# Attention and two feed-forward layers on one Trainium2 core: score and value matmuls chained in written order, transposes placed ahead of scores

## The chip, the core and the metric

The kernel runs on one core of one Trainium2 chip. The metric is the time of one execution on the device in microseconds (us), the median over a few runs. TensorE (PE) does the matmuls and the transposes and loads its weights beside them (PEld). VectorE (DVE), ScalarE (ACT) and GpSimd (POOL) do the elementwise work, and SyncE (SP) issues the DMAs.

## The reference

Three layers follow one another; each takes the output of the one before.

```python
# q, k, v: (4 batches, 8 heads, 576 positions, 64); positions of a batch see the last 128
scores = scale * np.matmul(q, k.transpose(0, 1, 3, 2))
mask = (rel >= 0) & (rel < 128)
scores = np.where(mask, scores + bias, -1e9)          # bias: slope of the head * distance
attn = np.exp(scores - max); attn = attn / (sum + 1e-9)
x = np.matmul(attn, v)                                # -> (2304 tokens, 512)
h = x @ w_in;  g = h * sigmoid(1.702 * h);  x = g @ w_out              # 512 -> 2048 -> 512
g = x @ w_gate; x = (g * sigmoid(g) * (x @ w_val)) @ w_out2            # 512 -> 1536 -> 512
```

## The kernel before

The 2304 tokens are 18 tiles of 128, taken in five blocks j of 4, 2, 4, 4 and 4 tiles (`A_BLOCKS`). A block goes through attention and then through the first feed-forward layer. The second layer follows for all tokens when the last block is done.

**Attention.** The eight heads are taken as four pairs `hp`; the two heads e of a pair lie in rows 0 to 63 and 64 to 127 of the q and k tiles. A group g is two token tiles. A unit (j, hp, g) has these steps:

- `scores`: 8 matmuls (16 instructions in the trace, two for each f32 matmul) into two PSUM banks `sb`, one for each head. From block 1 on each uses 64 rows and 64 columns of TensorE's array: the head sets the row half, the half c of the token tile sets the column half, so that four matmuls can stand on the array side by side.
- `minima` (DVE: the mask in `fold`, L365, then bias and minimum, L443), `exponentials` (ACT, L468), `reciprocals` (DVE), `normalise` (POOL, L491). The result is the tile `prob`; there are three of it.
- `transposes`: 4 matmuls with the identity into one bank `pt` (L536). `apart` copies it to `pf` (ACT, L567) and masks it in two selects (POOL, L569 and L572). There is one `pf`.

After both groups of a pair comes `values`: 24 matmuls (48 instructions) of `pf` and v. In blocks 2 to 4 they too are quarters of the array (L605): the half r of the keys sets the row half and the bank (`xb`, two of them), the head sets the column half. `take_x` adds the two banks (ACT L647, DVE L648) and splits the sum into `xh` and `xl` (L649, L641). In block 1 one bank and whole keys are used (L617).

**First feed-forward layer.** For each of 16 steps f of a block, `h_part` does 12 wide matmuls (128 x 512; 128 x 256 in block 1) into a bank `hp`, and ACT and DVE make `gh` and `gl` of it (L688, L690, L696, L698). `y_part`, two steps later, does 12 wide matmuls into four banks `y`, which the block holds to its end. Of the eight PSUM banks the four others go round among hp, sb, pt and xb.

**What sets the order.** Block 0 and the start of its layer follow a list, `PLAN`. From there on a loop over (j, f) issues `h_part`, an event, `y_part`, an event; an event of block j+1's attention has a place in half steps of block j (`hooks`). A unit's scores, its transposes and its pair's values have places of their own, worked out from `SPREAD`, `TRANSPOSE_LAG`, `VALUES_LAG` and `APART`. The rest is left to a scheduler: it orders each engine's instructions by its own estimates of time and may move a matmul whose inputs or bank it believes late behind others. `tc.issue_after(x)` forbids it to put an instruction ahead of x. Before the change the scores are behind the last h and y matmuls (`scores_and_norm`), and the first matmul of each triple in `three` is behind the last score matmul; the matmuls of a score unit and those of a value unit are not tied to each other.

The preparation of the second layer's weights (DMA, ACT, DVE; `prepare`) is issued in small steps between, in blocks 1 to 4.

## Time and profile before

| | |
|---|---|
| time, median of 3 runs | 903.93 us (903.85 to 904.41) |
| the profiled execution | 905.12 us, of which the span that the trace shows is 903.4 us |
| PE busy in the span | 890.8 us, 99% |
| DVE busy | 673.1 us, 75% |
| ACT busy | 453.9 us, 50% |
| attention of blocks 1 / 2 / 3 / 4 on PE | 72 to 130 / 130 to 195 / 195 to 302 / 302 to 396 us |
| second layer on PE | from about 500 us to the end |

A row of PE's timeline gives start and length of an instruction or of a run of equal ones; consecutive lengths overlap, since matmuls are pipelined. Starts are what counts: a wide matmul of 512 columns follows the one before at 0.23 us. So what a small unit costs PE is the time from the start of the last wide matmul ahead of it to the start of the first one behind it, less 0.23 us. A row's `[0.39 <-DVE th L690]` is idle time before it and what ended it.

### The profile page before, as it was taken

The page shows a single profiled execution, that of the slowest core. Times are in us where ns is not written, and L with a number is a line of the kernel's source. Part 1 is how long each engine was busy: PE and PEld are TensorE (multiplying, and loading weights), DVE is VectorE, ACT ScalarE, POOL GpSimd, SP SyncE. Part 2 cuts the span into 40 slices and gives each one's busy share as a digit, 9 for nine tenths or more (in the row PEclk, how much of TensorE's full clock was granted, in tenths as well). Part 3 has the DMA queues.
Part 4 walks back from the last instruction along what each step waited for, and adds up shares of the span by engine and source line. Part 5 has one row for each costly group of instructions (what it writes and reads, how often), then busy time and mean ns, then how long its engine had stood idle before and what let it go on. Part 6 is the DMA issues. An engine that isn't in the chain of part 4 may idle for free.

```text
span 903.4 us, 15609 instructions
## 1 busy us (share of the span) xinstructions
PE 890.8 (99%) x5556; PEld 794.4 (88%) x5556; DVE 673.1 (75%) x1707; ACT 453.9 (50%) x1065; POOL 119.4 (13%) x218
## 2 busy tenths in 40 slices
PE   7999999999999999999999999999999999999998
PEld 5687779987778776788888999999999999999998
DVE  8988847657776777877658386669866779866777
ACT  7867636645654555645445354435444335344331
POOL 6301413404440133210000000000000000000000
PEclk9999999999999999999999999999999999999999
DMA  9961214436455474546774577687887787887764
GB/s 332 377 246 29 72 56 147 153 108 199 169 194 197 165 237 163 207 162 234 249 300 146 209 263 268 245 305 260 289 292 257 255 315 260 289 293 258 258 223 140
DMA packets 71309, 199.20 MB, mean 220 GB/s; under 512 B 6720, under 2 KB 37952, under 8 KB 64320
## 3 DMA queue, kind: packets, MB, share of 16 engines
q1 hardware_dynamic: 71232, 198.21, 62.5%
q8 instruction: 44, 0.72, 0.3%
q14 instruction: 33, 0.27, 0.1%
HBM read 155.71 MB, written 42.47 MB: 219 GB/s over the span
## 4 chain that ended last, share of the span: by engine, by line
PE 82%; DVE 7%; DMA 6%; ACT 2%; issue 2%; SPq 1%; POOL 0%; DVEq 0%; ACTq 0%
PE sx L816 17%; PE ox L816 8%; PE sz L816 8%; PE y L653 6%; PE hp L653 6%; PE y L654 5%; PE y L655 5%; PE hp L654 5%; PE hp L655 5%; PE oz L816 4%; PE sy L816 4%; PE oy L816 2%; DMA wraw<-in_moe_w_in 2%; PE xb L605 2%; PE sb L395 1%
## 5 line engine op out<-in xcount | busy, mean ns | idle before, releaser
L816 PE MATMUL sx<-ya,wg 128*128 128x384 f32 x864 | 172.4, 335 | 0.0
L816 PEld LDWEIGHTS sx<-ya,wg 128*128 128x128 f32 x864 | 151.9, 188 | 0.1
L653 PE MATMUL hp<-xh,wt 128*128 128x512 f32 (+1 forms) x320 | 120.9, 378 | 0.6 <-DVE stat L443 0.3
L653 PE MATMUL y<-gh,wt 128*128 128x512 f32 (+1 forms) x320 | 120.4, 379 | 0.0
L654 PE MATMUL hp<-xl,wt 128*128 128x512 f32 (+1 forms) x320 | 118.2, 369 | 0.9 <-DVE xl L641 0.8
L655 PE MATMUL y<-gh,wt 128*128 128x512 f32 (+1 forms) x320 | 118.6, 371 | 0.0
L654 PE MATMUL y<-gl,wt 128*128 128x512 f32 (+1 forms) x320 | 118.2, 369 | 0.0
L655 PE MATMUL hp<-xh,wt 128*128 128x512 f32 (+1 forms) x320 | 117.9, 368 | 0.0
L816 PE MATMUL ox<-p,wg 128*128 128x384 f32 x432 | 89.6, 337 | 0.0
L845 DVE TENSOR_TENSOR p<-th,p 128x384 fp32r<-128x384 f32 x126 | 67.9, 552 | 28.2 <-ACT p L844 27.6
L816 PE MATMUL sz<-ya,wg 128*128 128x384 f32 x432 | 88.8, 336 | 0.0
L491 POOL TENSOR_SCALAR prob<-prob,stat 128x128 f32<-128x128 f32 x112 | 58.6, 539 | 179.2 <-DVE stat L481 60.8
L844 ACT ACTIVATE p<-th 128x384 fp32r<-128x384 f32 x126 | 63.4, 521 | 36.1 <-DVE th L840 28.5
L698 DVE TENSOR_TENSOR gl<-th,gh 128x512 fp32r<-128x512 f32 (+1 forms) x80 | 52.3, 654 | 33.2 <-ACT gh L696 32.1
L816 PEld LDWEIGHTS ox<-p,wg 128*128 128x128 f32 x432 | 76.5, 188 | 0.0
L816 PEld LDWEIGHTS sz<-ya,wg 128*128 128x128 f32 x432 | 76.1, 188 | 0.1
L653 PEld LDWEIGHTS y<-gh,wt 128*128 128x128 f32 x320 | 60.2, 188 | 14.4 <-issue 3.7
L653 PEld LDWEIGHTS hp<-xh,wt 128*128 128x128 f32 x320 | 60.1, 188 | 13.7 <-issue 1.7
L851 ACT ACTIVATE th<-c 128x384 f32<-128x384 f32 x54 | 28.3, 524 | 86.9 <-DVE c L836 86.7
L696 ACT ACTIVATE gh<-th 128x512 fp32r<-128x512 f32 (+1 forms) x80 | 46.8, 585 | 49.4 <-PE y L655 32.5
L654 PEld LDWEIGHTS hp<-xl,wt 128*128 128x128 f32 x320 | 60.2, 188 | 11.5 <-DVE xl L641 2.0
L655 PEld LDWEIGHTS hp<-xh,wt 128*128 128x128 f32 x320 | 60.1, 188 | 10.6 <-DVE wt L231 0.2
(112 smaller groups left out, 1558.3 us busy)
## 6 DMA issues: line engine op xcount, KB each, us to landing
wg<-w_scratch SPq DMA_DIRECT2D x36, 1024.0 KB, 5.4
wg<-w_scratch SPq DMA_DIRECT2D x36, 768.0 KB, 5.1
wg<-wo_scratch SPq DMA_DIRECT2D x18, 1024.0 KB, 6.6
wg<-wo_scratch SPq DMA_DIRECT2D x18, 768.0 KB, 7.9
w_scratch<-wa SPq DMA_DIRECT2D x24, 512.0 KB, 2.7
w_scratch<-wb SPq DMA_DIRECT2D x24, 384.0 KB, 3.5
wraw<-in_moe_w_in SPq DMA_DIRECT2D x16, 512.0 KB, 9.1
wraw<-in_moe_w_out SPq DMA_DIRECT2D x16, 512.0 KB, 9.4
```

What stands on the lines that cost most here:

```text
L395: ins = nc.tensor.matmul(out=sb[e][c : c + size, (i % 2) * 256 + lo : (i % 2) * 256 + hi], lhsT=u["q"][rows, i * P + c : i * P + c + size] ...
L491: nc.gpsimd.tensor_scalar(out=of[x], in0=of[x], scalar1=stat[:, 3, x : x + 1], scalar2=1.0, op0=ALU.mult, op1=ALU.mult,)
L605: nc.tensor.matmul(out=x[r][e * D : (e + 1) * D, i * P + a : i * P + a + w], lhsT=u["v"][e][keys, kt + lead, :], rhs=u["pf"][keys].rearran ...
L653: nc.tensor.matmul(out=out_ap, lhsT=whi, rhs=xhi, start=start, stop=False)
L654: nc.tensor.matmul(out=out_ap, lhsT=whi, rhs=xlo, start=False, stop=False)
L655: marks[products] = nc.tensor.matmul(out=out_ap, lhsT=wlo, rhs=xhi, start=False, stop=stop).ins
L696: a = nc.scalar.activation(out=gh[:, :m], in_=th[:, :m], func=AF.Copy)
L698: d = nc.vector.tensor_tensor(out=gl[:, :m], in0=th[:, :m], in1=gh[:, :m].bitcast(F32), op=ALU.subtract)
L816: nc.tensor.matmul(out=bank_[:, :HT], lhsT=w[:, kk, at, a, :], rhs=p2[2 * (q // 2 - 1) + kk, i][:, b, :] if m == "O" else y2[q // NP2, i][ ...
L844: nc.scalar.activation(out=t[:, 0], in_=src, func=AF.Copy)
L845: nc.vector.tensor_tensor(out=t[:, 1], in0=src, in1=t[:, 0].bitcast(F32), op=ALU.subtract)
L851: nc.scalar.activation(out=th, in_=g, func=AF.Tanh, scale=0.5)
```

## The change

Seven edits:

1. `in_row` ties each score and each value matmul of blocks 1 to 4 behind the one issued before it in the same unit.
2. The scores take the heads in turn, 1 then 0; the values take the key halves (and so the banks) in turn, 1 then 0, and the key tiles from the last to the first.
3. The first matmul of each h and y triple (`three`) is put behind the last value matmul too, not only behind the last score matmul.
4. The values are put behind the last h and y matmuls issued before them, as the scores are.
5. In blocks 3 and 4 (`JOINED`) the transposes are too, and
6. all places of these blocks come from a table, `PLACES`, one entry for each of 32 half steps: S is a unit's scores, T its transposes, V a pair's values. Unit n's transposes stand just ahead of unit n+2's scores.
7. In block 2 the values come 1.6 steps of the plan after the transposes, where it was 0.95.

```diff
@@ -78,6 +78,13 @@
 SPREAD, LOAD_LAG, TRANSPOSE_LAG, VALUES_LAG, APART = 0.65, 0.3, 4.0, 0.95, 2.0
 
 LENGTHS = {1: 8, 2: 18}
+
+JOINED = 3, 4
+
+PLACES = (
+    "", "S0", "", "S1", "", "", "", "T0 S2", "", "T1 S3", "", "V0", "", "T2 S4", "", "T3 S5", "", "V1",
...
+)
 
 QUARTERS = 1, 2
 
@@ -373,6 +380,13 @@
 
         return range(2 * g, min(2 * g + 2, a_blocks[j][1]))
 
+    def in_row(j, prev, matmul, **kw):
+
+        if j == 0:
+            return matmul(**kw).ins
+        with tc.issue_after(prev) if prev is not None else nullcontext():
+            return matmul(**kw).ins
+
     def scores(j, hp, g):
 
 
@@ -383,6 +397,7 @@
         sb = [bank("sb") for _ in range(2)]
         quarters = j >= QUARTERS[0]
         size = D if quarters else P
+        ins = None
         for i in tiles:
             for c in range(0, P, size):
 
@@ -390,16 +405,19 @@
                 if c and kind(t0 + i) == "cross":
                     lo = P + D
                 hi = P + c + size
-                for e in range(2):
+                for e in range(2) if j == 0 else (1, 0):
                     rows = slice(e * D, (e + 1) * D)
-                    ins = nc.tensor.matmul(
+                    ins = in_row(
+                        j,
+                        ins,
+                        nc.tensor.matmul,
                         out=sb[e][c : c + size, (i % 2) * 256 + lo : (i % 2) * 256 + hi],
                         lhsT=u["q"][rows, i * P + c : i * P + c + size],
                         rhs=u["k"][rows, (i + lead - 1) * P + lo : (i + lead - 1) * P + hi],
                         start=True,
                         stop=True,
                         skip_group_check=quarters,
-                    ).ins
+                    )
         if j > 0:
             marks["sb"] = ins
         u["sb", g] = sb
@@ -584,7 +602,9 @@
         def row(e, i):
             return 2 * (4 * (i // 2) + e * len(tiles_of(j, i // 2)) + i % 2)
 
-        for kt in range(-lead, n):
+        order = range(-lead, n) if j == 0 else range(n - 1, -lead - 1, -1)
+        ins = None
+        for kt in order:
             qts = [i for i in (kt, kt + 1) if 0 <= i < n and (i == kt or kind(t0 + i) != "first")]
             if quarters:
 
@@ -597,31 +617,39 @@
                 together = len(qts) == 2 and kt % 2 == 0
                 for p in range(1 if together else len(qts)):
                     for e in range(2):
-                        for r in range(2):
+                        for r in (1, 0):
                             (i, own, a, b), last = parts[r][p], parts[r][-1 if together else p]
                             w = b - a if last[0] == i else P - a + last[3]
                             at = (row(e, i) + own) * P + a
                             keys = slice(r * D, (r + 1) * D)
-                            nc.tensor.matmul(
+                            ins = in_row(
+                                j,
+                                ins,
+                                nc.tensor.matmul,
                                 out=x[r][e * D : (e + 1) * D, i * P + a : i * P + a + w],
                                 lhsT=u["v"][e][keys, kt + lead, :],
                                 rhs=u["pf"][keys].rearrange("p x c -> p (x c)")[:, at : at + w],
-                                start=(kt == -lead and p == 0),
-                                stop=(kt == n - 1),
+                                start=(kt == order[0] and p == 0),
+                                stop=(kt == order[-1]),
                                 skip_group_check=True,
                             )
                 continue
             w = len(qts) * P
             for e in range(2):
                 rows = [row(e, i) + (i == kt) for i in qts]
-                nc.tensor.matmul(
+                ins = in_row(
+                    j,
+                    ins,
+                    nc.tensor.matmul,
                     out=x[0][e * D : (e + 1) * D, qts[0] * P : qts[0] * P + w],
                     lhsT=u["v"][e][:, kt + lead, :],
                     rhs=u["pf"][:, rows[0] : rows[-1] + 1 : max(1, rows[-1] - rows[0]), :],
-                    start=(kt == -lead),
-                    stop=(kt == n - 1),
+                    start=(kt == order[0]),
+                    stop=(kt == order[-1]),
                     skip_group_check=True,
                 )
+        if j > 0:
+            marks["xb"] = ins
         u["x"] = x
 
     def take_x(j, hp, lower):
@@ -649,7 +677,10 @@
         nc.scalar.activation(out=xh[:, hp, :m], in_=total[:, :m], func=AF.Copy)
 
     def three(products, out_ap, whi, wlo, xhi, xlo, start, stop):
-        with tc.issue_after(marks["sb"]) if "sb" in marks else nullcontext():
+        with ExitStack() as behind:
+            for row in ("sb", "xb"):
+                if row in marks:
+                    behind.enter_context(tc.issue_after(marks[row]))
             nc.tensor.matmul(out=out_ap, lhsT=whi, rhs=xhi, start=start, stop=False)
         nc.tensor.matmul(out=out_ap, lhsT=whi, rhs=xlo, start=False, stop=False)
         marks[products] = nc.tensor.matmul(out=out_ap, lhsT=wlo, rhs=xhi, start=False, stop=stop).ins
@@ -935,12 +966,17 @@
         normalise(*u)
 
     def transposed(*u):
-        transposes(*u)
+        if u[0] in JOINED:
+            with tc.issue_after(marks["h"]), tc.issue_after(marks["y"]):
+                transposes(*u)
+        else:
+            transposes(*u)
         for select in range(2):
             apart(*u, select)
 
     def values_and_x(j, hp):
-        values(j, hp)
+        with tc.issue_after(marks["h"]), tc.issue_after(marks["y"]):
+            values(j, hp)
         for lower in range(2):
             take_x(j, hp, lower)
 
@@ -1048,6 +1084,21 @@
 
         if j > 1:
             ev.append((at - 1, start))
+        if j in JOINED:
+            for n, place in enumerate(PLACES):
+                for what in place.split():
+                    h = int(what[1:])
+                    if what[0] == "V":
+                        ev.append((at + n, lambda h=h: values_and_x(j, h)))
+                        continue
+                    u = j, h // G, h % G
+                    if what[0] == "T":
+                        ev.append((at + n, lambda u=u: transposed(*u)))
+                        continue
+                    ev.append((at + n, lambda u=u: scores_and_norm(*u)))
+                    if h % G == G - 1 and h // G + 2 < H // 2:
+                        ev.append((at + n + 1, lambda h=h: load_pair(j, h // G + 2)))
+            return [(min(p, 2 * begin[j] - 1), e) for p, e in ev]
         begun, scored, valued = 0, 0, []
         for h in range(G * H // 2):
             u = j, h // G, h % G
@@ -1062,7 +1113,7 @@
             begun = max(begun, at + step * h + lag)
             ev.append((begun, lambda u=u: transposed(*u)))
             if last:
-                begun = begun + step * VALUES_LAG
+                begun = begun + step * (VALUES_LAG if j != 2 else 1.6)
                 valued.append(begun)
                 ev.append((begun, lambda u=u: values_and_x(*u[:2])))
         return [(min(p, 2 * begin[j] - 1), e) for p, e in ev]
```

On PE, the value unit of block 3's third pair before the change (xb_3326 is the bank of key half 0, xb_3327 that of half 1, pf the masked weights, y and hp the wide matmuls of the first layer):

```order
L605 MATMUL xb_3326<-pf_3133,vr_2635 64x64 [waits DMAHW0_49,DVE_49,Pool_49]
L605 MATMUL xb_3326<-pf_3133,vr_2635 64x192 [waits Pool_49]
L605 MATMUL xb_3326<-pf_3133,vr_2635 64x192
...
L605 MATMUL xb_3326<-pf_3133,vr_2635 64x128 x2
L653 MATMUL y_2659<-gh_3159,wt_842 128x512
...
L654 MATMUL y_2661<-gl_3160,wt_842 128x512
L605 MATMUL xb_3327<-pf_3133,vr_2635 64x128 [waits DVE_49,PE_49]
L605 MATMUL xb_3327<-pf_3133,vr_2635 64x192 x2
...
L605 MATMUL xb_3327<-pf_3133,vr_2635 64x64 x2
L536 MATMUL pt_3357<-ident_70,prob_3193 128x128 [waits DVE_49,PE_49,Pool_49]
```

All twelve matmuls of half 0 stand together, eight wide ones come, and then the twelve of half 1. The same unit with the change (xb_3392 is half 1, xb_3391 half 0):

```order
L686 MATMUL y_2653<-gh_3197,wt_836 128x512
L388 MATMUL xb_3392<-pf_3224,vr_2635 64x64 [waits DMAHW0_49,Activation_49,Pool_49]
L388 MATMUL xb_3391<-pf_3224,vr_2635 64x128 [waits DVE_49,PE_49]
L388 MATMUL xb_3392<-pf_3224,vr_2635 64x64 [waits DMAHW1_49]
L388 MATMUL xb_3391<-pf_3224,vr_2635 64x128
L388 MATMUL xb_3392<-pf_3224,vr_2635 64x192
L388 MATMUL xb_3391<-pf_3224,vr_2635 64x192
...
L388 MATMUL xb_3391<-pf_3224,vr_2635 64x64
L684 MATMUL hp_3429<-xh_1826,wt_1009 128x512 [waits DVE_49,PE_49]
```

The 24 stand together, the halves in turn, and the first waits for the last select on POOL and for both banks.

On PE, a score unit of block 4 before (sb_4264 and sb_4265 are the banks of its two heads):

```order
L655 MATMUL y_3897<-gh_4023,wt_704 128x512
L395 MATMUL sb_4264<-kr_3869,qr_3868 64x192 [waits DVE_49]
L395 MATMUL sb_4264<-kr_3869,qr_3868 64x192 x3
L395 MATMUL sb_4265<-kr_3869,qr_3868 64x192 [waits Activation_49]
L395 MATMUL sb_4265<-kr_3869,qr_3868 64x192 x3
L653 MATMUL y_3894<-gh_4112,wt_577 128x512
```

One head's four matmuls stand ahead of the other's. The same unit with the change, with the transposes (pt) that the table places there:

```order
L686 MATMUL y_3888<-gh_4105,wt_577 128x512
L554 MATMUL pt_4308<-ident_70,prob_4059 128x128 [waits Activation_49,Pool_49]
L554 MATMUL pt_4308<-ident_70,prob_4059 128x128 [waits Pool_49] x3
L388 MATMUL sb_4317<-kr_3869,qr_3868 64x192 [waits DVE_49,PE_49]
L388 MATMUL sb_4316<-kr_3869,qr_3868 64x192 [waits DVE_49,PE_49]
L388 MATMUL sb_4317<-kr_3869,qr_3868 64x192
L388 MATMUL sb_4316<-kr_3869,qr_3868 64x192
...
L388 MATMUL sb_4316<-kr_3869,qr_3868 64x192
L684 MATMUL y_3885<-gh_4191,wt_729 128x512
```

The transposes of the unit two before stand directly ahead, and the two heads come in turn. The matmuls of the second layer stand on PE in the same order before and after.

## Rows read from the trace of the kernel before

**Rows 1.** The page: busy time (part 1), shares of the chain that ended last (part 4).

```profile
PE 890.8 (99%) x5556; PEld 794.4 (88%) x5556; DVE 673.1 (75%) x1707; ACT 453.9 (50%) x1065; POOL 119.4 (13%) x218
...
PE 82%; DVE 7%; DMA 6%; ACT 2%; issue 2%; SPq 1%; POOL 0%; DVEq 0%; ACTq 0%
```

**Rows 2.** Windows by stage: length, busy us of PE, PEld, DVE, ACT, POOL; clock, DMA.

```profile
195.00:302.00 107.00, 106.61 (x737) 84.44 (x736) 78.44 (x257) 57.96 (x156) 31.44 (x48) 1.00 0.55 187
302.00:396.00 94.00, 91.75 (x657) 70.84 (x655) 73.61 (x250) 53.94 (x148) 27.15 (x48) 1.00 0.56 192
396.00:903.00 507.00, 503.84 (x2754) 484.51 (x2748) 370.27 (x739) 218.63 (x443) 0.00 (x0) 1.00 0.72 253
```

**Rows 3.** PE's timeline, two score units: start us, length us, line, out<-in, form, count.

```profile
195.67 0.88 PE L395 MATMUL sb<-kr,qr 64*64 64x192 f32 x16
...
349.59 0.39 PE L655 MATMUL y<-gh,wt 128*128 128x512 f32 x1
349.91 0.89 PE L395 MATMUL sb<-kr,qr 64*64 64x192 f32 x16
350.73 0.50 PE L653 MATMUL y<-gh,wt 128*128 128x512 f32 x1
```

**Rows 4.** PE's timeline, a score unit of block 3 with a late second head.

```profile
237.27 0.39 PE L655 MATMUL y<-gh,wt 128*128 128x512 f32 x1
238.05 1.45 PE L395 MATMUL sb<-kr,qr 64*64 64x192 f32 x16 [0.39 <-DVE th L690]
239.42 0.50 PE L653 MATMUL hp<-xh,wt 128*128 128x512 f32 x1
```

**Rows 5.** PE's timeline, a value unit of block 3 in one piece.

```profile
282.18 1.55 PE L605 MATMUL xb<-pf,vr 64*64 64x64 f32 x48
```

**Rows 6.** PE's timeline, a value unit of block 3 in two pieces.

```profile
264.29 1.54 PE L605 MATMUL xb<-pf,vr 64*64 64x64 f32 x24
...
267.82 1.53 PE L605 MATMUL xb<-pf,vr 64*64 64x128 f32 x24
```

**Rows 7.** Windows of the value matmuls L605 alone, blocks 2, 3 and 4.

```profile
130.00:195.00 65.00, 6.50 (x192) 5.16 (x192) 1.00 0.39 127
195.00:302.00 107.00, 8.20 (x192) 7.11 (x192) 1.00 0.55 187
302.00:396.00 94.00, 8.13 (x192) 7.06 (x192) 1.00 0.56 192
```

**Rows 8.** Windows of the score matmuls L395 alone, blocks 3 and 4.

```profile
195.00:302.00 107.00, 8.11 (x128) 5.00 (x128) 1.00 0.55 187
302.00:396.00 94.00, 7.82 (x128) 4.75 (x128) 1.00 0.56 192
```

**Rows 9.** PE's timeline, two places of block 1's attention.

```profile
109.30 1.09 PE L617 MATMUL xb<-pf,vr 128*64 128x128 f32 x12
110.32 0.66 PE L536 MATMUL pt<-ident,prob 128*128 128x128 f32 x4
...
114.56 0.44 PE L617 MATMUL xb<-pf,vr 128*64 128x128 f32 x4
114.93 0.66 PE L536 MATMUL pt<-ident,prob 128*128 128x128 f32 x4
115.52 0.87 PE L395 MATMUL sb<-kr,qr 64*64 64x192 f32 x8
116.31 0.87 PE L617 MATMUL xb<-pf,vr 128*64 128x256 f32 x8
...
117.91 0.50 PE L653 MATMUL y<-gh,wt 128*128 128x512 f32 x1
```

**Rows 10.** Transposes of block 4 on PE, and the last select of their copy (POOL).

```profile
337.88 0.66 PE L536 MATMUL pt<-ident,prob 128*128 128x128 f32 x4
...
345.62 0.63 POOL L572 TENSOR_SCALAR_AFFINE_SELECT pf<-pf 128x512 f32<-128x512 f32 x1
```

More of the change, by code (lines that the diff above doesn't have):

```diff
@@ L80 @@
 LENGTHS = {1: 8, 2: 18}
+JOINED = 3, 4
+PLACES = (
+    "", "S0", "", "S1", "", "", "", "T0 S2", "", "T1 S3", "", "V0", "", "T2 S4", "", "T3 S5", "", "V1",
+    "", "T4 S6", "", "T5 S7", "", "V2", "", "T6", "", "T7", "", "V3", "", "",
+)
 QUARTERS = 1, 2
```

## The prediction, made before the changed kernel ran

> **What bounds the kernel now.** I began with the page's busy times and its chain of waits. PE is busy for 890.8 of 903.4 us, and 82% of the chain that ended last are PE's own instructions; DVE comes next with 7% [rows 1]. So a change pays only where it shortens what PE does or the few waits in which PE stands still. Next the windows by stage: behind the last attention unit, from 396 us on, PE stands still for 3 of 507 us, and its order there isn't changed; the change acts in the attention of blocks 1 to 4. In block 3 PE idles for 0.39 us, in block 4 for 2.25 us [rows 2]. Little of the loss is idle time, then. The rest hides in "busy" PE, and only the timeline shows it: the small matmuls of one unit cost different times at different places.
>
> A score unit of 16 instructions lasts 0.88 or 0.89 us; it costs PE 350.73 - 349.59 - 0.23 = 0.91 us [rows 3]. Another, 237.27 to 239.42, costs 1.92 us: PE waited 0.39 us at its start, and then it lasted 1.45 us [rows 4]. A value unit of 48 instructions in one piece lasts 1.55 us [rows 5]. In two pieces of 24 the pieces last 1.54 and 1.53 us, as much each as the whole [rows 6]. A piece holds one key half, so it uses one row half of the array, and nothing stands on the other. That is what the reader is to see: the same count of instructions, and twice the time.
>
> **The change part by part.** No matmul is added or taken away. What changes is which ones stand side by side, and what waits.
>
> *Values of blocks 3 and 4 (edits 1 to 4).* All value matmuls of block 3 take 8.20 us, of block 4 8.13 us [rows 7]. Four whole units would take 4 x 1.55 = 6.20 us. That gives 2.00 + 1.93 = 3.9 us. Each block has one unit in two pieces; its second piece enters the small form once more, and a small unit begins 0.32 us after the wide matmul ahead of it (349.59 to 349.91) instead of 0.23 [rows 3], so 2 x 0.1 = 0.2 us more. Together 4.1 us. This gain is certain as far as the units stand together in the new order, and they do. The reversed key order costs nothing by itself: as many matmuls of the same widths.
>
> *Values of block 2.* 6.50 - 6.20 = 0.3 us [rows 7]; the last but one unit stands in three pieces, two entries more, 0.2 us. Together 0.5 us.
>
> *Block 1.* A value unit (4 of 12 instructions), transposes, 8 score instructions, the other 8 of the values, the other 8 of the scores take 117.91 - 114.56 = 3.35 us. The scores of one head alone take 0.79 us (115.52 to 116.31), as much as both together. Joined: values 1.02 (109.30 to 110.32), transposes 0.59 (114.93 to 115.52) [rows 9], scores 0.82 (349.91 to 350.73) [rows 3], in all 2.43 us. Gain 0.9 us.
>
> So far 4.1 + 0.5 + 0.9 = 5.5 us.
>
> *Scores: the heads in turn.* In 13 of the 28 units before, one head's matmuls stand ahead of the other's in the queue. That costs nothing as long as both banks are free: the unit at 349.91 is one of these, with 0.89 us, the one at 195.67 has the heads in turn, with 0.88 [rows 3]. I take 0. The Trainium skill ("TensorE: Matmul & The Clock Gate", Part 3, "What overlaps and what doesn't") says the opposite: "MATMULs are pc-monotone in start AND end — strict FIFO, no reordering", by which the second head couldn't start beside the first, and taking turns would be worth a lot. Here the trace disagrees with it, 0.89 against 0.88 us; it is the last rival below.
>
> *Waits that the old order has.* Score matmuls take 8.11 and 7.82 us in blocks 3 and 4 [rows 8], eight clean units 8 x 0.89 = 7.12: 0.99 + 0.70 = 1.7 us lie in units whose second head waited for its bank. With PE's idle 0.39 + 2.25 = 2.6 us [rows 2] there are 4.3 us of waiting.
>
> *Waits that the new order has.* Here the trace of before shows only neighbours. Each place in blocks 3 and 4 is fixed now, and PE takes its queue in order: behind a late unit stand the wide matmuls of h, which feed ACT and DVE. Four banks still serve hp, pt, sb and xb, so a score unit still asks for two banks that DVE has to give back; I let the 1.7 us stay. The transposes come six half steps behind their scores, some 17 us (a half step is 94 us / 32 = 2.9 us [rows 2]), and shouldn't wait. The values are new: their first matmul asks for the last select and both banks, where the old order began with what was there. Between the end of the transposes and the values now stand a score unit and 24 wide matmuls, 0.8 + 24 x 0.23 = 6.3 us. In the trace the select after the transposes at 337.88 ended at 346.25, 7.7 us behind their end [rows 10]. That was with other work ahead of the copy on ACT, and it would be 1.4 us late. The lower bound is 0. I take 0.1 us for each of 8 units, near the lower end, as the copy stands early on ACT in the new order: 0.8 us. New waits in all 1.7 + 0.8 = 2.5 us, between 0 and 1.7 + 12 x 1.4 = 18.5.
>
> *Transposes directly ahead of scores.* Only an entry into the small form could be spared, 0.1 us for each of 12 at most, while transposes followed by scores take 0.59 us [rows 9]. I take 0, bounds -1.2 and +1.2 us.
>
> *DMA.* The next pair's q, k and v are asked for at other places on SP, and the v load waits until the values have read the old tile; the raw weights queue behind it. Today that is hidden: the view of waits names no DMA among PE's in blocks 3 and 4, and DVE, which works on the raw weights, is busy for only 73.61 of 94 us [rows 2]. I take 0; if this cover is gone, the first layer's ACT work comes late, which is rival 2.
>
> **Sum.** -5.5 - 4.3 + 2.5 = -7.3 us. The profiled execution took 905.12 us, the span and 1.7 us around it; it is 1.2 us above the median of the runs, and I apply the difference to that median: 903.9 - 7.3 = 896.6 us.
>
> **The rivals.**
>
> 1. All waits go, as the table gives every step more time than it has now. For it: a late head is rare, 1.7 us over 16 units. Against it: no bank is added. 903.9 - 5.5 - 4.3 = 894.1 us.
> 2. DVE keeps what PE saves. It is busy for 78% of block 4's time; with 5 us less that is 83%, and in order. If half of the gain in blocks 3 and 4 (4.1 + 4.3 - 2.5 = 5.9 us) comes back as waits of PE, 899.6 us; if all of it, 902.5 us, and only blocks 1 and 2 have gained.
> 3. Slower: PE stands before the value units until the last select is done. If ACT's copy is as late as at 337.88, that is 1.4 us for each of 12 units, 17 us: 903.9 - 9.8 + 17 = 911 us. It decides from 9.8 / 12 = 0.8 us for each unit. For it: that row is no mishap but a copy queued behind DVE-fed work. Against it: that place had an exponential and the halves of x ahead of the copy.
> 4. The heads in turn pay as well: if the first head's matmuls really kept the second's out, a unit would go from about 1.55 us (the length of a one-half piece [rows 6]) to 0.89, and 13 units would give 8.6 us more: 888.0 us. The rows speak against it.
>
> **How the numbers follow.** The forecast 45%, rival 1 25%, rival 2 21% (13% half, 8% all), rival 3 7%, rival 4 2%. About 0.2%, 1.8 us, is what a measurement of this kernel can tell from no change. Below 902.1 us lie the forecast, rivals 1 and 4, and rival 2 where it keeps half: 85%, and a little of its other case: 86%. Same 7%, slower 7%. The likeliest case by itself spans 895 to 899 us (waits between 1 and 5 us); the range goes from 891 us, rival 1 with 1.2 us from the transposes and some of rival 4, to 901 us, rival 2 between its cases.
>
> **What would show it.** Right: each value unit of blocks 2 to 4 one run of 48 with some 1.55 us, so about 6.2 us a block; scores near 7.1 to 8 us a block; no score matmul between two value runs in block 1; the second layer as long as before. Wrong: value units one run but with idle time ahead that a POOL select or a DVE minimum ended (rival 3); wide h matmuls that wait for ACT or DVE more than now (rival 2); block lengths unchanged though the small units have shrunk.

## The result and the profile after

| | time, us | runs | ratio to before, with interval |
|---|---|---|---|
| before, beside the first runs of after | 904.35 (903.85 to 905.17) | 6 | |
| after | 896.21 (894.07 to 899.29) | 6 | 0.991 (0.9887 to 0.9933) |
| before, beside the second runs | 905.09 (904.52 to 905.8) | 7 | |
| after, the same kernel again | 896.65 (894.28 to 897.19) | 4 | 0.9901 (0.9886 to 0.9916) |

The change makes the kernel about 8 us faster; 896.6 us was forecast. The first six runs of after fall into two groups, 894.07 to 894.79 us and 897.63 to 899.29 us, three each, and the median is the middle of the gap between them. The profile after is of the run of 894.27 us, of the shorter group, and that matters below. The page's busy time of PE, answering to [rows 1]:

```profile
PE 883.8 (99%) x5556; PEld 792.8 (89%) x5556; DVE 672.0 (75%) x1707; ACT 455.7 (51%) x1065; POOL 121.7 (14%) x218
```

PE is as full as before (99%), but with 7.0 us less work in it. The windows by stage (length, busy us of PE, PEld, DVE, ACT, POOL; clock, DMA share, GB/s), answering to [rows 2]:

```profile
195.00:295.00 100.00, 100.00 (x722) 80.44 (x720) 78.07 (x253) 57.78 (x154) 30.94 (x48) 1.00 0.56 193
295.00:390.00 95.00, 95.00 (x645) 75.36 (x644) 77.30 (x261) 58.38 (x155) 25.39 (x46) 1.00 0.58 204
390.00:892.60 502.60, 498.99 (x2769) 480.45 (x2768) 367.19 (x729) 215.94 (x439) 1.47 (x2) 1.00 0.71 253
```

In the attention of blocks 3 and 4 PE doesn't stand still at all now, where it idled for 0.39 and 2.25 us. DVE is a little fuller, 78% and 81% of the two windows instead of 73% and 78%, and PE waits for it nowhere in them. In the window behind the attention PE idles for 3.6 us, before 3.2.

PE's timeline of block 3, a value unit and a joined pair of transposes and scores, answering to [rows 3 to 6]:

```profile
226.60 0.39 PE L686 MATMUL hp<-xh,wt 128*128 128x512 f32 x1
226.91 1.58 PE L388 MATMUL xb<-pf,vr 64*64 64x64 f32 x48
228.43 0.50 PE L684 MATMUL hp<-xh,wt 128*128 128x512 f32 x1
...
233.77 0.39 PE L686 MATMUL y<-gh,wt 128*128 128x512 f32 x1
234.00 0.60 PE L554 MATMUL pt<-ident,prob 128*128 128x128 f32 x4
234.53 0.88 PE L388 MATMUL sb<-kr,qr 64*64 64x192 f32 x16
235.34 0.50 PE L684 MATMUL hp<-xh,wt 128*128 128x512 f32 x1
```

The value unit is one run of 48 with 1.58 us; from the wide matmul ahead of it (226.60) to the one behind (228.43) it costs 1.83 - 0.23 = 1.60 us. No unit of blocks 2 to 4 is in pieces any more. Transposes and scores together cost 235.34 - 233.77 - 0.23 = 1.34 us; the scores by themselves last 0.88 us, as when nothing is late.

The value tiles alone, by block (2, 3, 4), the first number behind the length PE's, answering to [rows 7]; and the same for the scores of blocks 3 and 4, answering to [rows 8]:

```profile
127.00:191.60 64.60, 5.89 (x192) 5.22 (x192) 5.83 (x9) 4.74 (x8) 1.00 0.41 133
191.60:295.00 103.40, 6.32 (x192) 5.64 (x192) 5.54 (x8) 4.73 (x8) 1.00 0.55 191
295.00:401.90 106.90, 6.32 (x192) 5.64 (x192) 5.41 (x8) 4.74 (x8) 1.00 0.58 204
```

```profile
191.60:295.00 103.40, 7.00 (x128) 4.11 (x128) 16.15 (x72) 1.00 0.55 191
295.00:401.90 106.90, 7.26 (x128) 4.41 (x128) 15.59 (x72) 1.00 0.58 204
```

Values fell from 6.50, 8.20 and 8.13 us to 5.89, 6.32 and 6.32, scores from 8.11 and 7.82 to 7.00 and 7.26. The 0.2 us by which block 4's scores exceed block 3's are its last unit, of 1.09 us. In block 2 the scores became longer, by 0.6 us: its last two units now read

```profile
158.35 1.05 PE L388 MATMUL sb<-kr,qr 64*64 64x192 f32 x16
167.65 1.39 PE L388 MATMUL sb<-kr,qr 64*64 64x192 f32 x16
```

where they lasted 0.89 and 0.79 us (159.35 and 166.77 in the trace before). In block 1 the place of [rows 9] now reads, in PE's timeline:

```profile
114.18 0.39 PE L686 MATMUL hp<-xh,wt 128*128 128x512 f32 x1
114.50 1.09 PE L388 MATMUL xb<-pf,vr 128*64 128x128 f32 x12
115.52 0.66 PE L554 MATMUL pt<-ident,prob 128*128 128x128 f32 x4
116.10 0.88 PE L388 MATMUL sb<-kr,qr 64*64 64x192 f32 x16
116.91 0.50 PE L684 MATMUL y<-gh,wt 128*128 128x512 f32 x1
```

Values, transposes and scores stand one behind the other: 116.91 - 114.50 = 2.41 us, where it was 3.35.

The last select behind one pair of transposes, and these transposes and the value unit on PE, answering to [rows 10]:

```profile
245.72 1.05 POOL L590 TENSOR_SCALAR_AFFINE_SELECT pf<-pf 128x512 f32<-128x512 f32 x1
```

```profile
240.92 0.60 PE L554 MATMUL pt<-ident,prob 128*128 128x128 f32 x4
...
247.92 1.58 PE L388 MATMUL xb<-pf,vr 64*64 64x64 f32 x48
```

The select ends at 246.77, 5.25 us behind the transposes' end at 241.52, the latest of the 16 in blocks 3 and 4 (the others 2.0 to 5.1 us). The values start at 247.92: nothing waits, and 1.15 us is the least that any of the eight units has to spare.

Where the time went, by the first h matmul of each block in every profile (us, each bound read to 0.1; a column is the stage in which PE does that block's attention between the wide matmuls; the experiments stand beside, for later):

| kernel | attention 1 | 2 | 3 | 4 | rest of block 4's layer | second layer |
|---|---|---|---|---|---|---|
| before | 103.0 | 64.8 | 107.3 | 112.6 | 89.8 | 400.9 |
| after, 894.27 us | 101.7 | 64.6 | 103.4 | 106.9 | 89.7 | 401.0 |
| after again, 896.28 us | 102.0 | 64.6 | 103.4 | 106.9 | 91.5 | 401.0 |
| ties alone | 101.8 | 68.7 | 107.7 | 116.6 | 89.8 | 400.9 |
| places alone | 102.8 | 64.5 | 104.2 | 109.0 | 91.6 | 401.0 |
| ties, values later | 107.7 | 66.2 | 109.1 | 114.7 | 90.7 | 401.0 |
| values nearer | 102.2 | 64.6 | 107.1 | 113.3 | 89.7 | 401.2 |
| heads apart | 107.3 | 64.6 | 103.4 | 109.1 | 91.6 | 400.9 |
| key halves apart | 102.2 | 67.4 | 106.6 | 110.1 | 91.3 | 400.9 |
| scores first | 102.1 | 64.7 | 103.0 | 107.2 | 89.7 | 401.0 |
| keys first to last | 102.7 | 64.6 | 103.4 | 106.8 | 90.1 | 401.0 |
| splits later by one | 101.9 | 64.6 | 103.3 | 106.7 | 90.4 | 400.9 |
| splits later by two | 101.8 | 64.6 | 103.4 | 106.7 | 89.9 | 401.0 |

The gain lies in blocks 3 and 4 (3.9 and 5.7 us) and in block 1 (1.3). The two runs of after differ by more than 0.3 us in one column alone, by 1.8 us, behind the last attention.

### The profile page after: what moved, and what is told of

It is laid out like the page before. It is cut to its first block, busy times and chain, and to the rows that moved or that the text cites. A ratio compares the mean times of both kernels' runs of the same rounds, so it can differ in the third digit from the quotient of the medians.

```text
span 892.6 us, 15625 instructions
## 1 busy us (share of the span) xinstructions
PE 883.8 (99%) x5556; PEld 792.8 (89%) x5556; DVE 672.0 (75%) x1707; ACT 455.7 (51%) x1065; POOL 121.7 (14%) x218
## 4 chain that ended last, share of the span: by engine, by line
PE 93%; DVE 5%; POOL 1%; issue 1%; ACT 0%; DVEq 0%; POOLq 0%; ACTq 0%
PE sx L847 17%; PE ox L847 8%; PE sz L847 8%; PE y L684 7%; PE hp L684 7%; PE y L686 7%; PE y L685 7%; PE hp L685 7%; PE hp L686 7%; PE oz L847 4%; PE sy L847 4%; PE xb L388 2%; PE sb L388 2%; PE oy L847 2%; PE pt L554 1%; DVE cv L228 1%
## 5 line engine op out<-in xcount | busy, mean ns | idle before, releaser
L509 POOL TENSOR_SCALAR prob<-prob,stat 128x128 f32<-128x128 f32 x112 | 56.8, 525 | 183.0 <-DVE stat L499 116.3
```

What stands on the lines that cost most here:

```text
L509: nc.gpsimd.tensor_scalar(out=of[x], in0=of[x], scalar1=stat[:, 3, x : x + 1], scalar2=1.0, op0=ALU.mult, op1=ALU.mult,)
```

## The experiments

The theory: side-by-side units and fewer waits make the gain; the new order's own waits were the unknown. The rivals: the ties make PE stand before late values (rival 3), or the ties bring nothing beside the places. Each experiment is timed beside the kernel before on the same chip.

**1. The ties without the places (edits 1 to 4).** `values(j, hp)` is tied as after the change; the places are those of before.

```diff
-JOINED = 3, 4
+JOINED = ()
-                begun = begun + step * (VALUES_LAG if j != 2 else 1.6)
+                begun = begun + step * VALUES_LAG
```

> Edits 1 to 4 alone (score and value matmuls tied in turn, values behind h and y); the places are those of before. Theory A (what the change brings is mostly that every value unit stands in one piece): the value matmuls fall to about 6.3 us a block and the scores' mix in block 1 goes, 5.5 us, while the waits of the old places stay: 904.3 - 5.5 = 898.8 us, range 897 to 901. Rival T (it is the table of places, which gives every step time): the ties alone make PE wait at the old, closer places, and the time stays within 902 to 905 us.

Measured: 914.01 us (911.86 to 916.13), ratio 1.0095 (1.0079 to 1.0111): slower than before by 8.4 us. PE's waits from 72 us on (us in all, times, longest), the two that count:

```profile
PE xb L388 <- DVE stat L461: 5.8, 2, 3.1
PE xb L388 <- POOL pf L590: 3.2, 1, 3.2
```

The timeline of two of the three places, and the windows behind the first and around the second (columns as above, the clock behind POOL):

```profile
269.82 1.54 PE L388 MATMUL xb<-pf,vr 64*64 64x128 f32 x46 [2.68 <-DVE stat L461]
...
380.94 0.33 PE L388 MATMUL xb<-pf,vr 64*64 64x64 f32 x2
384.42 2.58 PE L388 MATMUL xb<-pf,vr 64*64 64x128 f32 x46 [3.15 <-DVE stat L461]
```

```profile
269.80:273.20 3.40, 3.38 (x57) 3.07 (x58) 2.28 (x9) 2.81 (x11) 1.47 (x5) 1.00 0.57 194
381.00:384.40 3.40, 0.27 (x3) 0.14 (x3) 2.90 (x13) 1.43 (x3) 0.58 (x2) 1.00 0.29 115
384.70:388.10 3.40, 3.40 (x50) 3.28 (x42) 1.91 (x5) 2.10 (x10) 1.34 (x4) 0.50 0.65 228
```

The first two instructions of the unit run in the first bank, the third asks for the second, and PE stands for 3.15 us until DVE's minima give it back. So the first matmul of a unit doesn't wait for both banks, as was written ahead of the runs; each bank is waited for by the first matmul that writes it. Everything behind is tied. In the stretch behind it the granted clock is 0.50, the lower of its two levels (1.2 GHz), and the 46 take 2.58 us. There were three such waits, 9.0 us: 3.20 us ahead of a unit of block 2, for the last select, and 2.68 and 3.15 us for the second bank in blocks 3 and 4. Three stretches of half clock followed, but not one behind each: there is none behind the wait of 2.68 us (first window), and one from 350.60 us on, behind waits of 0.65 and 0.82 us. This is the sign that the prediction gave for rival 3, at the places of before; both theories put the time too low.

**2. The places without the ties (edits 5 to 7).** `in_row`, the new marks and the turns are taken back.

```diff
-        with tc.issue_after(marks["h"]), tc.issue_after(marks["y"]):
-            values(j, hp)
+        values(j, hp)
-                for e in range(2) if j == 0 else (1, 0):
-                    ins = in_row(j, ins, nc.tensor.matmul, ...
+                for e in range(2):
+                    ins = nc.tensor.matmul(...
```

> Edits 5 to 7 alone: the table of places for blocks 3 and 4 with the transposes behind h and y, and the later values of block 2; no ties within units, heads and halves in the old order, values free to move. Its program order shows the value units of blocks 2 to 4 whole, some with a run of 3 to 5 of one half ahead, and the mix of block 1 as before. Theory A with the table: values 4.6 us and most of the 4.3 us of waits gone, block 1's 0.9 us not: 904.3 - 8 = 896 to 898 us. If the ties are what takes the waits away, only the 4.6 us go: 899 to 900 us.

Measured: 901.93 us (899.56 to 905.42), ratio 0.996 (0.9949 to 0.9971). The score tiles in blocks 3 and 4:

```profile
192.10:296.30 104.20, 7.48 (x128) 4.59 (x128) 16.74 (x72) 1.00 0.56 189
296.30:405.30 109.00, 8.80 (x128) 5.69 (x128) 15.74 (x72) 1.00 0.57 199
```

Both forecasts were too low; that of 899 to 900 us, by which the ties take the waits away, is the nearer. The value units of blocks 3 and 4 are whole here too (1.55 to 1.71 us): the places alone bring that. What is missing to the change in the profiled runs lies in scores with a late second head (7.48 and 8.80 us, after 7.00 and 7.26), in block 1 (1.1 us) and behind the attention (1.9 us); the last is not of the ties, for the changed kernel has it too in its second profile. Each against its own runs of before, the places alone are 3.7 us faster (905.65 to 901.93) and the change 8.1 (904.35 to 896.21). So the ties cost 8.4 us without the places and bring 4.4 with them.

**3. The ties, and later values in the planner's places.** Is it the place of the values alone that makes experiment 1 slow?

```diff
-                begun = begun + step * VALUES_LAG
+                begun = begun + step * 1.6
```

> The run with the ties alone (914.0 us), with one number more: the values of all of blocks 1 to 4 stand 1.6 steps behind their transposes instead of 0.95 (the change does that for block 2 alone); the table isn't used, so block 3 and 4's units stand in the planner's own places. Theory A: what made the ties alone slow was the places of the values, 9.2 us of PE idle ahead of three units and half-clock stretches behind each; with later places both go, and the time is 914.0 - 9.2 - 3 x 1.7 = 899.7 us, between 897 and 902, the rest to the changed kernel being late second heads of the scores. Rival T: the ties keep PE waiting whatever the places; above 906 us.

Measured: 911.12 us (908.68 to 916.29), ratio 1.0071 (1.0045 to 1.0097). Theory A, 899.7 us, falls. The profile is of the longest run. PE's waits:

```profile
PE pt L554 <- DVE stat L461: 5.4, 2, 3.0
PE xb L388 <- DVE th L721: 3.6, 4, 1.3
PE xb L388 <- POOL pf L590: 2.2, 1, 2.2
```

The values' wait for the second bank is gone (5.8 us in experiment 1) and that for the select smaller, but transposes now wait for DVE to give back a bank of scores, 5.4 us, and values for one that DVE has last to read for h, 3.6. Four banks go round, and here a unit moved alone handed its wait to its neighbour. The run doesn't price this cleanly. It moves block 1's values too, which the change doesn't do, and block 1's stage is 5.9 us longer than with the ties alone (107.7 against 101.8). The granted clock was 0.50 for 17 us of the profiled run, while the runs with 1.0 throughout took 908.68 and 908.85 us. But blocks 3 and 4 are 5.7 and 7.8 us longer than with the change (109.1 and 114.7 against 103.4 and 106.9). Rival T has the time right, above 906 us, though not its "whatever the places": with the table's places the waits are gone. What the table does is to place scores, transposes and values together.

**4. The values one half step nearer to their transposes**, in the change's table:

```diff
-    "", "S0", "", "S1", "", "", "", "T0 S2", "", "T1 S3", "", "V0", "", "T2 S4", ...
+    "", "S0", "", "S1", "", "", "", "T0 S2", "", "T1 S3", "V0", "", "", "T2 S4", ...
```

> The changed kernel with each value unit of blocks 3 and 4 one half step (some 2.9 us) nearer to its transposes: some 3.6 us behind their end instead of 6.5. The last select of the eight units was ready 3.0, 5.3, 4.2, 3.0, 4.7, 3.8, 5.1 and 3.0 us behind the transposes' end in the changed kernel. Theory A (PE stands before a value unit until the last select is done, rival 3's mechanism): waits of about 0, 1.7, 0.6, 0.1, 1.1, 0.2, 1.5 and 0.2 us, 5.4 us in all, so 901.6 us, between 899 and 904, with idle of PE ahead of the value units that ends with the POOL select. Rival B: DVE and ACT move along with PE, and the select comes as much earlier: 896.2 us as the changed kernel.

Measured: 901.84 us (901.11 to 905.07), ratio 0.9971 (0.9961 to 0.9982); 901.6 was expected by theory A, 896.2 by the rival. PE's waits in blocks 3 and 4, and one unit:

```profile
PE xb L388 <- POOL pf L590: 3.8, 6, 1.2
PE xb L388 <- DVE stat L461: 3.3, 3, 1.8
```

```profile
224.55 0.33 PE L388 MATMUL xb<-pf,vr 64*64 64x64 f32 x2
226.17 1.54 PE L388 MATMUL xb<-pf,vr 64*64 64x128 f32 x46 [1.30 <-DVE stat L461]
```

Half of it is the select, as theory A has it; the other half is the second bank, which theory A left out, so its number is partly luck. The profiled run is the longest, 905.07 us, with 7.1 us of such waits. Beside the kernel before (904.82 us) 3.0 us of gain are left. So the new order's freedom from waits hangs on one half step: 2.9 us nearer gives back 5 of the 8 us.

**5. The heads one behind the other**, all else as changed (head 1's score matmuls, then head 0's, tied).

```diff
-        for i in tiles:
-            for c in range(0, P, size):
-                for e in range(2) if j == 0 else (1, 0):
+        for e, i, c in [(e, i, c) for e in (1, 0) for i in tiles for c in range(0, P, size)]:
```

> The changed kernel, but a score unit's matmuls are tied with head 1's four ahead of head 0's four. Theory A (PE lets the second head's matmuls start beside the first's as long as both are in its queue and their banks are free): the scores last as long as with the heads in turn, 0.88 to 0.90 us a unit, 896 us. Rival F (matmuls start strictly in program order, so that a head's own half blocks the other): each of 28 units lasts about 1.55 us instead of 0.88, 18 us more, 914 us.

Measured: 904.85 us (900.47 to 909.96), ratio 0.9991 (0.9975 to 1.0007). The score tiles in blocks 3 and 4:

```profile
198.00:301.40 103.40, 7.12 (x128) 4.36 (x128) 16.85 (x72) 1.00 0.57 190
301.40:410.50 109.10, 9.30 (x128) 6.10 (x128) 15.71 (x72) 1.00 0.58 200
```

In block 3 taking turns is worth nothing: 7.12 us against 7.00, and the stage lasts 103.4 us in both. In block 4 four units last 1.28 to 1.75 us, and its scores take 2.0 us more than in the changed kernel. The largest part, 5.6 us, is block 1's: there the scheduler put transposes among the scores and PE waits once for 3.11 us for the select behind them, with the granted clock at 0.50 in the stretch that follows. That part says nothing on the turns, and so the run doesn't price them. Why the second head is late in block 4 with the heads apart (here and in experiment 2), while the changed kernel shows only one long unit there, of 1.09 us, and no idle time, stays open.

**6. The key halves one behind the other**, all 24 instructions of half 1 and then 24 of half 0, in one tied run.

```diff
-        for kt in order:
+        for kt, half in [(kt, half) for half in ((1, 0) if quarters else (None,)) for kt in order]:
-                        for r in (1, 0):
+                        for r in (half,):
```

> The changed kernel, but a value unit of blocks 2 to 4 has its twelve matmuls of key half 1 ahead of the twelve of half 0, in one run, with nothing between. Theory A (standing in one run is enough): 1.55 to 1.65 us a unit as in turn, 896 us. Rival F (strict order): 3.0 us a unit, 12 units, 17 us more, 913 us. In between, if PE looks only some matmuls ahead: part of the second half runs beside the first.

Measured: 904.54 us (903.51 to 905.96), ratio 0.9989 (0.9981 to 0.9998). A unit of block 3 in PE's timeline:

```profile
229.55 2.38 PE L388 MATMUL xb<-pf,vr 64*64 64x64 f32 x48
```

2.38 us against 1.58 with the halves in turn; in block 2 it is 2.16 against 1.47. Twelve units give 9.1 us, the values of the three blocks 27.6 - 18.5, and the stages of blocks 2 to 4 are longer by 2.8, 3.2 and 3.2 us. So the price of halves apart is shown by itself, and it takes 7 of the change's 8 us. It is not what the change gained, though: before it only three of the twelve units were in pieces, and the values of these blocks gave 22.8 - 18.5 = 4.3 us.

Instruction by instruction the trace shows where the overlap begins. In all twelve units the first instruction of half 0 starts right behind the eighteenth of half 1's 24, in this unit 0.84 us behind the start, when six are left; from there on the two run side by side. In experiment 5 the second head of every unit of blocks 2 to 4 that wasn't late starts right behind the second of the first head's eight, again with six left, 0.03 us behind the start. That fits four and four matmuls one behind the other losing nothing and twelve and twelve losing 0.8 us a unit; a late bank would not strike at the same instruction every time.

**7. Scores ahead of the transposes** in blocks 3 and 4.

```diff
-    ..., "T0 S2", "", "T1 S3", "", "V0", "", "T2 S4", "", "T3 S5", ...
+    ..., "S2 T0", "", "S3 T1", "", "V0", "", "S4 T2", "", "S5 T3", ...
```

> Blocks 3 and 4 with each score unit ahead of the transposes that stand beside it, where the change has the transposes ahead (12 places). Theory A (position is free, as the prediction had it): the same time as the changed kernel, 896.2 us, within 1.2. Rival S: the 0.6 us of the transposes is time in which DVE gives back the second bank; ahead of them the second head's scores stand late by 0.3 to 0.5 us at each of 12 places, 4 to 6 us more, 900 to 902 us, and the score units of blocks 3 and 4 last 1.2 to 1.4 us instead of 0.88.

Measured: 896.67 us (894.3 to 898.87), ratio 0.9905 (0.9887 to 0.9923). Rival S falls: the order of the two is free within what can be told.

**8. The key tiles first to last**, as before the change.

```diff
-        order = range(-lead, n) if j == 0 else range(n - 1, -lead - 1, -1)
+        order = range(-lead, n)
```

> The changed kernel with the key tiles of a value unit taken first to last, as before the change, in blocks 1 to 4. Theory A (the reversal is free): 896.2 us, within 1.2. Rival K: the last key tiles' probabilities come last or first out of the selects, so that one of the two orders waits for its second select; each of 16 value units then waits up to 0.6 us longer, up to 10 us in all, with idle time of PE ahead of or inside the value units that ends with the POOL select.

Measured: 897.32 us (895.47 to 897.89), beside 896.65 us of the changed kernel (894.28 to 897.19) on the same chip; ratio 0.991 (0.9895 to 0.9925) against 0.9901. Value units last 1.55 us instead of 1.58, none waits, and block 1 is 0.7 to 1.0 us longer, as one of its value units stands in two pieces again, with transposes and scores between (114.76 and 116.18). Rival K falls; a difference below 1 us can't be told.

**9. Where the changed kernel's scatter comes from.** Its runs spread over 894 to 899 us, those of before beside them over 1.3 us; its 28 and 17 runs beside experiments 1 and 3 spread over 3.3 and 3.7 us. The kernel once more:

> The changed kernel itself once more, with another profile. Theory A (its scatter is the wait of ACT for the first y quarter, which PE feels only where the quarter lands late): the runs scatter from 894 to 899 us again, and if the profiled run is a long one, its excess lies behind block 4's middle, as PE's idle time ahead of y matmuls. Rival: the excess of a long run lies elsewhere, in the first 25 us or in the attention of blocks 1 to 4.

Measured: 896.65 us; the profiled run took 896.28 us. Here are ACT's and PE's timelines behind block 4's middle, in this run:

```profile
458.58 0.85 ACT L783 ACTIVATE ya<-yr 128x768 fp32r<-128x768 f32 x1 [4.66 <-DMA yr<-y_scratch]
459.33 0.61 ACT L727 ACTIVATE gh<-th 128x512 fp32r<-128x512 f32 x1
```

```profile
460.00 0.50 PE L684 MATMUL y<-gh,wt 128*128 128x512 f32 x1 [0.28 <-ACT gh L727]
461.07 0.50 PE L685 MATMUL y<-gl,wt 128*128 128x512 f32 x1 [0.57 <-DVE gl L729]
```

And ACT's in the run of 894.27 us:

```profile
456.59 0.85 ACT L783 ACTIVATE ya<-yr 128x768 fp32r<-128x768 f32 x1 [4.88 <-DMA yr<-y_scratch]
457.34 0.61 ACT L727 ACTIVATE gh<-th 128x512 fp32r<-128x512 f32 x1
```

The first split of the second layer's input, `ya`, waits 4.7 or 4.9 us on ACT for a DMA, and `gh` of block 4's layer stands behind it on that engine. In the run of 894.27 us `gh` started 55.4 us into the block (457.34 - 401.9) and PE never noticed; in this one 57.2 us in (459.33 - 402.1), and PE stood for 0.28 and 0.57 us. SP had issued the DMA 49.4 us into the block there (451.33) and 50.9 us in here (452.97). The stage is 1.8 us longer, 0.9 us of it idle time of PE. Places alone, heads apart and key halves apart have the same idle, 0.96 to 1.18 us, and the same long stage in the table above.

**10. The splits later by one step, and by two.**

```diff
-        if j == na - 1 and f >= CLOSE:
+        if j == na - 1 and f >= CLOSE and f != CLOSE + 1:                    # by one
+        if j == na - 1 and f >= CLOSE and f not in (CLOSE + 1, CLOSE + 2):   # by two
             in_order(first)
```

> One step of the next layer's ACT work (the splits of y) is left out at the second half step pair after block 4's middle, so every later step of it comes one pair (5.7 us) later; nothing else differs from the changed kernel. Theory A: the changed kernel's own scatter (894.1 to 899.3 us in six runs) comes from ACT standing in order before a y quarter whose DMA has not landed: gh is then late and PE waits some 2 to 3 us. Then these runs all stand near 894 us, within 1.5 us of each other, and the two idle times of PE near 464 and 469 us are below 0.1 us. Rival: the scatter has another cause; then the runs scatter over 894 to 899 as before, median 896.

> The changed kernel with the next layer's ACT work left out at two half step pairs behind its first (the kernel with one left out ran 895.1 to 896.3 us, and its profiled run still had 0.23 us of PE idle ahead of a y matmul, 3.12 us of ACT's before the first split). Theory A: no idle of PE ahead of y matmuls, the runs within 1.5 us of each other, median 895.0, between 894 and 896.3. Rival: the scatter is not there; 896.2 us with a scatter of 4 us and more.

Measured: by one 895.88 us (895.09 to 896.27), ratio 0.9895 (0.988 to 0.9909); by two 894.78 us (893.97 to 895.34), ratio 0.9887 (0.9871 to 0.9904). ACT in the second:

```profile
453.96 0.58 ACT L719 ACTIVATE th<-hp 128x512 f32<-128x512 f32 x1
456.16 0.63 ACT L727 ACTIVATE gh<-th 128x512 fp32r<-128x512 f32 x1 [1.62 <-PE y L686]
458.89 0.85 ACT L783 ACTIVATE ya<-yr 128x768 fp32r<-128x768 f32 x1 [2.10 <-DMA yr<-y_scratch]
```

The `gh` now stands ahead of the split, the split still waits for the DMA, and no y matmul waits for ACT. With the step later by one a y matmul still waited for 0.23 us. The runs, five and four, lie within 1.2 and 1.4 us, as theory A had it; the level of the first (894 expected) was missed by 1.9. By two is the fastest version here; beside the changed kernel on the same chip it is 1.9 us ahead in the median, with intervals that overlap. So the wait and its 1.8 us are shown; that it makes the whole scatter, or its upper end of 899.3 us, is not, since the longest runs have no profile and before scatters by 3.7 us too where it ran more often.

## Why the prediction was right, and where not

896.6 us was forecast, 896.21 and 896.65 came. That the medians are so close is luck; the range and the direction are not. By its steps:

- *Side by side, -5.5 us: right in size, not all of it by that cause.* Values of blocks 3 and 4 gave 8.20 + 8.13 - 6.32 - 6.32 = 3.7 us for 3.9; block 2's 0.6 for 0.3; block 1's place 0.94 for 0.9. But only 3.0 of the 3.9 us were the units in two pieces (1.54 + 1.53 - 1.55 in each block). The rest was one unit in each block that stood whole and still lasted 2.03 and 2.06 us; why is not shown. In the trace before the first reads

```profile
245.09 2.03 PE L605 MATMUL xb<-pf,vr 64*64 64x64 f32 x48
```

  The prediction gave this gain to the ties; experiment 2 has whole units without them. Block 2's stage is only 0.2 us shorter, since its late scores took the gain back.
- *Old waits, -4.3 us: right.* Scores 1.67 us (8.11 + 7.82 - 7.00 - 7.26), PE's idle 2.6.
- *New waits, +2.5 us: wrong in size and in place.* In blocks 3 and 4 PE's idle time is 0. I let the 1.7 us of late second heads stay because no bank is added; 0.2 us of them are left there, and block 2, for which I had no such term, has 0.6. The 0.8 us ahead of the values are not there either: the select is up to 5.25 us behind the transposes, not 7.7, since ACT's copy starts up to 1.7 us behind them, not 5.7. What held it at 337.88 was less the exponential and the halves of x than a step of the weight preparation ahead of it on ACT, which waited for DVE:

```profile
343.21 0.66 ACT L246 ACTIVATE cs<-raw 128x512 f32<-128x512 f32 x1 [2.71 <-DVE wb L256]
```

  With 0.8 us of late heads in place of 2.5 this comes near rival 1, whose 894.1 us the run of 894.27 meets.
- *DMA, 0: wrong.* The term looked at q, k, v and the raw weights, not at the y quarters. Block 4's layer starts 10.8 us sooner than before (401.9 against 412.7), the first y quarter is asked for only 8.7 us sooner (451.3 against 460.0), and ACT's wait for it costs 1.8 us in the run of 896.28. This and the waits that stayed away are of opposite sign, and so the median met the forecast; how much of the 3 to 5 us between the two groups of runs it makes is open.
- *Blocks 3 and 4 gave 9.7 us in the profiled run,* 8.4 by the terms without new waits. Counted from start to start the 9.7 are values 3.7, scores 1.9, idle time 2.6 and wide matmuls 2.7, less 1.2 that the transposes cost more, directly ahead of scores. The term that is missing is the change of form. PE goes from wide to small matmuls 35 times before and 28 times after, and as many wide matmuls, nearly all of them the second behind a small group, follow the one before at 0.31 us or more instead of 0.23; the prediction had only the entry, 0.1 us, and only for the value units in pieces.
- *Rival 2 didn't come:* PE waits nowhere in blocks 3 and 4, though DVE is busy for 81% of block 4's window.
- *Heads in turn, 0: right where both banks are free* (block 3, 7.12 against 7.00), not shown in block 4, where the two kernels with heads apart are 1.5 and 2.0 us longer in their scores. So rival 4's gain of 0.66 us a unit isn't there in block 3. Of the Trainium skill's rule in "TensorE: Matmul & The Clock Gate", Part 3, strict order in start and end: 16 instructions of two heads one behind the other take 0.89 us as those in turn do, so there it doesn't hold; but 24 and 24 of the key halves take 2.38 us, between 1.58 in turn and 3.07 as two separate pieces [rows 6], as the second half starts only behind the eighteenth of the first (experiment 6).
- *Transposes ahead of scores, 0: right for the order of the two* (896.67 against 896.21); what joining them is worth was not run by itself. The reversed key order costs nothing within what can be told.
- *Rival 3 was the real danger.* PE standing before value units is what makes the ties alone slow by 8.4 us, with 2.7 to 3.2 us at each of three places rather than 1.4 at twelve, at one of them for the select, as rival 3 has it, and at two for the second bank. Stretches at half clock, which no rival had, come on top. The table keeps clear of it by 1.15 us at the tightest place; experiment 4 moves inside that and pays.

## What to carry to other kernels

In this kernel it paid to tie small matmuls that can stand side by side on the array in the order that fills it, but only together with places at which their last input and their second bank are ready: the ties alone lost 8.4 us, with the places they won 4.4 more than the places did. Before tying, read from the trace how far the last producer ends behind its trigger, and leave that much work and a margin between. When a stage gets shorter, look for work on another engine that stands behind a wait for a DMA with a time of its own: here it was the next thing that was late.

## What the runs showed of the hardware

- After PE had stood for 3.15 us in the ties alone, the granted clock was 0.50 (1.2 GHz) in the stretch behind; after 2.68 us in the same run it was not. Waits of 1.3 us (226.17) and others below 1.8 us in experiment 4 were followed by no such stretch, while in experiment 3 one stood behind a wait of 1.39 us in block 1. So the length of the wait alone doesn't settle it.
- Two runs of 24 small matmuls on different row halves, one behind the other in one tied unit, overlap in part: 2.38 us, not 3.07 and not 1.58. The second run's first matmul started when six instructions of the first were left, in twelve units of twelve, and with runs of eight likewise, in all sixteen units that weren't late.
- The first two wide matmuls behind a group of small ones start 0.31 to 0.34 us apart, in all 28 places of blocks 3 and 4 after the change; wide matmuls otherwise follow at 0.23 us.
